# Overlapping the seams of a three-stage kernel: filter stage laid into the last spectrum pass, first parameter block laid into the last output pass

## The chip, the cores and the metric

One core of a Trainium2 chip runs the kernel. The metric is device microseconds of one execution. Engines are named as in the profile: PE is TensorE (PEld its weight loads), DVE VectorE, ACT ScalarE, POOL GpSimd, SP SyncE. A run counts as *slow* when it is over 1.5% above the fastest of the same kernel, else as *fast*.

## The reference, cut to what matters

The function mixes two branches of a sequence `x` of 2048 x 1024 by a gate and returns the output and all gradients.

```python
g = sigmoid((x * gate_w).sum(-1, keepdims=True))
a = irfft2(rfft2(x) * (w_r + 1j * w_i))                 # spectral branch
K = einsum("dn,dnl,dn->dl", C, exp(dt * A * l), dt * B).real
b = irfft(rfft(pad(x)) * rfft(pad(K)))[:L] + x * Dskip  # long convolution
out = g * a + (1 - g) * b
# returned: out and the gradients of x, w, A, B, C, log_dt, Dskip, gate_w for a given grad_out
```

The part of the kernel that the change touches has three stages. The *spectrum* of the convolution kernels is made in four passes, the last at about 875 to 905 us. The *filter* stage then runs over eight blocks of 128 channels: a second transform of the data, products with the spectrum, an inverse transform, one big transpose of the tile `Vt` into `Vr`, and an output pass. The *parameter* stage reduces the lag correlations that the filter stage left (`GKall`) to the gradients of A, B and C.

## The kernel before

The kernel is written with pools of buffers and a scheduler that orders each engine's instructions. Each engine is given its own list and waits on semaphores. The parts that matter, with cuts marked:

```python
# spectrum: all passes run with filler=None, the filter's pools open after the last one
if bi % 2 == 1:
    spectrum(bi // 2, Kc, K0, None)
...
for g0, g1 in ((0, 4), (4, 8), (8, 12), (12, 17)):       # 5.4 MB of tables, GpSimd's queue
    nc.gpsimd.dma_start(out=TKT[:, g0:g1]..., in_=tkt_scr[...])
...
def first(pr_, h, fp_, pool, tag, nb, eng):               # 24 of 64 are left for this stage
    if h % 2 == 0:
        xg = fp_.tile([P, 2, 2, 256], dt.bfloat16, name="xg", bufs=2)
        nc.sync.dma_start(out=xg[:, :, 0, :], in_=xv3[...])
        nc.sync.dma_start(out=xg[:, :, 1, :], in_=gbv[...])
    ...                                                   # 2 matmuls, one eviction to st, a store
...
sgs = {(0, g): load_s(0, g) for g in range(3)}
lts = {(0, hq): fetch(0, hq) for hq in range(4)}          # 12 output loads, 3.1 MB
for bi in range(DC):                                      # 8 filter blocks
    for g in range(NG):                                   # 5 groups
        nxt = second(...)                                 # group one ahead
        PY = products(g, *cur)
        firsts(1)
        lags(bi, *pend, pq)
        inverse(g, PY, Vt)
        firsts(1)
        last(bi - 1, Vr, g, ...)                          # outputs of the block before
    turn(Vr, Vt)                                          # the big transpose
for g in range(4):
    last(DC - 1, Vr, g, ...)
...                                                       # grad_s, pools closed, tail's pools opened
cur = blk_in(0)                                           # diagonal tile BD (4 copies on ACT)
for ch in range(4):
    blk_ch(0, ch, *cur)                                   # 16 matmuls, evictions to Tsb on ACT
load_par()                                                # four loads, the gate's row gwb last
for bi in range(DC):                                      # pd = Tsb * ORJ on DVE, pr = sums on PE
    ...
```

A *first* is the first transform of one slice of `x` and its gradient, two matmuls for a later block: Sync loads its input pair `xg`, its result is stored and read back as `Sg` by a *second*. `XG` is the output of a second, `PY` a product with the spectrum. `BD` is the diagonal tile made from one block of `GKall`; it is multiplied with four loaded chunks `A2t`, and an *eviction* copies each result out of TensorE's result memory (PSUM) to `Tsb`.

## Time and profile before

Median 1482.71 us of three runs (1478.46 to 1489.49); the span of the profiled execution, a further one, was 1489.8 (timed at 1491.57). I cut everything after the last small transpose of the lag rows (`KT<-Kq`) into four stretches, bounded by that transpose, the first and the last big transpose of the filter stage (`Vr<-Vt`), the first big product of the parameter stage (`pd`), and the end.

| stretch | us | what it holds |
|---|---|---|
| start of the program to the lag rows | 873.2 | not touched by the change |
| lag rows to first big transpose | 87.6 | first seam |
| first to last big transpose | 285.1 | seven filter blocks |
| last big transpose to first product | 59.5 | second seam |
| first product to end | 184.4 | the tail |

The same stretches in the busy times of the profile before (bounds, length, then busy time and instructions of PE, PEld, DVE, ACT, POOL; granted clock, DMA share, GB/s):

```profile
873.17:960.78 87.61, 61.75 (x422) 42.47 (x423) 36.22 (x82) 32.60 (x40) 15.84 (x17) 0.80 0.70 246
960.78:1245.87 285.09, 242.11 (x1726) 173.19 (x1725) 250.97 (x535) 162.70 (x270) 48.70 (x67) 0.92 0.74 144
1245.87:1305.40 59.53, 22.07 (x121) 12.58 (x119) 27.21 (x33) 31.16 (x60) 20.47 (x27) 0.65 0.88 254
1305.40:1489.80 184.40, 135.70 (x1200) 107.88 (x1199) 158.70 (x140) 114.65 (x153) 20.95 (x39) 0.90 0.53 177
```

Read DVE (third number) against the length: 36 of 88, 251 of 285, 27 of 60, 159 of 184. VectorE is nearly full in the second and fourth stretch, and the first and third, the seams, are mostly waiting. What a reordering can win lies mainly there.

### The profile page before, as it was taken

How to read it: one execution, taken by the hardware profiler on the slowest of the kernel's cores; microseconds unless marked ns; L12 is line 12 of the kernel's file. 1: busy time of each engine (PE TensorE's matmuls, PEld its weight loads, DVE VectorE, ACT ScalarE, POOL GpSimd, SP SyncE). 2: the span in 40 equal slices, each digit the busy share in tenths (PEclk: the TensorE clock that was granted, in tenths of full speed). 3: DMA queues.
4: the chain of work that ended last, by engine and by line, in shares of the span. 5: the costliest groups of instructions: out<-in, count | busy, mean ns of one | idle time of the engine just before them, and what ended most of it. 6: DMA issues, size and time to landing. Idle time of an engine off the chain costs nothing. (4 is left out here: it accounts for less than half of the span.)

```text
span 1489.8 us, 20203 instructions
## 1 busy us (share of the span) xinstructions
PE 1077.9 (72%) x7161; PEld 736.3 (49%) x7187; DVE 1133.5 (76%) x1883; ACT 857.4 (58%) x1321; POOL 237.8 (16%) x493
## 2 busy tenths in 40 slices
PE   3968887688790558757758773989888886387883
PEld 1434454344450445546546652656656654165672
DVE  5668998476628888687788853669989997378997
ACT  3553455433358785786784631757555554587860
POOL 4101100021243211010100104001212031321010
PEclk9979999899995557656858776989999998589996
DMA  4446574257535333344433538959986655877641
GB/s 148 152 139 157 154 233 151 100 118 117 83 129 224 117 132 133 116 157 168 154 124 120 184 106 310 268 128 171 190 143 161 84 187 76 316 248 258 205 148 29
DMA packets 153067, 236.06 MB, mean 158 GB/s; under 512 B 26371, under 2 KB 100739, under 8 KB 149766
## 3 DMA queue, kind: packets, MB, share of 16 engines
q1 hardware_dynamic: 133190, 179.37, 44.7%
q0 software_dynamic: 13536, 53.84, 10.4%
q10 hardware_dynamic: 6240, 1.57, 0.5%
q8 instruction: 56, 0.92, 0.3%
q14 instruction: 45, 0.37, 0.1%
HBM read 126.80 MB, written 107.66 MB: 157 GB/s over the span
## 5 line engine op out<-in xcount | busy, mean ns | idle before, releaser
L888 PE MATMUL pK<-wO,AN 128*128 128x84 bf16 x512 | 101.2, 344 | 24.3 <-DVE st L996 22.3
L1068 ACT ACTIVATE Vt<-f 128x1024 bf16<-128x1024 f32 (+1 forms) x72 | 64.4, 929 | 82.1 <-PE f L1157 44.9
L887 PE MATMUL trp<-ident,AN 128*128 128x128 bf16 x512 | 75.9, 275 | 47.8 <-DVE AN L817 41.5
L1309 ACT ACTIVATE Tsb<-pT 128x704 bf16<-128x704 f32 x128 | 88.0, 754 | 37.8 <-PE pT L1308 33.8
L1383 DVE TENSOR_TENSOR pd<-Tsb,ORJt 128x5376 bf16<-128x5376 bf16 x32 | 94.3, 2952 | 9.5 <-PE pr L1389 6.1
L923 PE MATMUL kx<-Kc,TK 128*128 128x256 bf16 x680 | 98.5, 291 | 0.7 <-DVE Kc L910 0.6
L888 PEld LDWEIGHTS <-AN 128*128 128x128 bf16 x512 | 75.6, 151 | 30.7 <-issue 25.3
L887 PEld LDWEIGHTS <-AN 128*128 128x128 bf16 x512 | 60.6, 158 | 55.5 <-DVE AN L817 42.9
L551 PE MATMUL p<-TD,UV 128*128 128x512 bf16 x240 | 66.9, 404 | 25.3 <-DVE Y L555 16.8
L1166 PE MATMUL pq<-TKT,PY 128*128 128x321 bf16 x544 | 83.7, 301 | 1.3 <-DVE PY L1136 1.0
L1308 PE MATMUL pT<-BD,A2t 128*128 128x176 bf16 x512 | 59.3, 251 | 31.3 <-ACT BD L1295 17.0
L1068 ACT ACTIVATE XG<-f 128x1024 bf16<-128x1024 f32 (+1 forms) x72 | 68.3, 984 | 19.7 <-PE f L1104 5.7
L1389 PE MATMUL pr<-pd,ident 128*128 128x256 bf16 x504 | 66.9, 281 | 16.9 <-DVE pd L1383 12.8
L923 PEld LDWEIGHTS <-TK 128*128 128x128 bf16 x680 | 64.1, 103 | 19.9 <-issue 2.6
L1123 DVE TENSOR_TENSOR m<-XG,kb 128x1024 bf16<-128x1024 bf16 (+1 forms) x80 | 47.0, 605 | 34.9 <-ACT XG L1068 21.0
L1193 PE MATMUL f<-Vr,S1i 128*128 128x256 bf16 x256 | 68.7, 391 | 4.2 <-DVE Vr L1074 4.2
L631 PE MATMUL p2i<-T,Z 128*128 128x512 bf16 x224 | 60.9, 394 | 12.8 <-DVE Z L598 5.9
L1308 PEld LDWEIGHTS <-A2t 128*128 128x128 bf16 x512 | 45.0, 102 | 49.1 <-issue 43.0
L1166 PEld LDWEIGHTS <-PY 128*128 128x128 bf16 x544 | 52.7, 98 | 25.2 <-DVE PY L1136 3.0
L996 DVE CAST st<-pK 128x1024 bf16<-128x1024 f32 x40 | 48.6, 1218 | 19.8 <-PE pK L991 19.7
L1389 PEld LDWEIGHTS <-ident 128*128 128x128 bf16 x504 | 49.3, 100 | 25.9 <-issue 11.6
L494 PE MATMUL p<-DP,UV 128*128 128x512 bf16 x250 | 61.1, 385 | 0.6 <-DVE UV L640 0.3
(829 smaller groups left out, 3160.7 us busy)
## 6 DMA issues: line engine op xcount, KB each, us to landing
at<-A SPq DMA_DIRECT2D x32, 512.0 KB
st<-st SPq DMA_DIRECT2D x64, 256.0 KB
A2t<-at SPq DMA_DIRECT2D x32, 512.0 KB
Sg<-st SPq DMA_DIRECT2D x24, 512.0 KB
on_scr<-OP SPq DMA_DIRECT2D x8, 1344.0 KB
ORJt<-on_scr POOLq DMA_DIRECT2D x8, 1344.0 KB, 8.9
spk<-spk SPq DMA_DIRECT2D x64, 128.0 KB
kb<-spk SPq DMA_DIRECT2D x32, 256.0 KB
```

Source lines behind the costliest of these rows:

```text
L494: nc.tensor.matmul(pd[:, eo, :], lhsT=V[:, eo * 2 + c_, b_, :, :].rearrange("p k n -> p (k n)")[:, h::H16], rhs=DP[:, eo * 2 + c_, b_, :], ...
L551: nc.tensor.matmul(ps[:, eo, :], lhsT=U[:, dc, (eo * K16 + k1r) * P:(eo * K16 + k1r + 1) * P], rhs=TD[:, dc, eo, :], start=(dc == 0), stop ...
L887: nc.tensor.transpose(trp[:, comp, cc, :], AN[:, comp, :, c], ident[:, :])
L888: nc.tensor.matmul(pK[:, c4, cc * 4 * NA:(cc + 1) * 4 * NA], lhsT=AN[:, comp, :, c], rhs=wO[:, comp, :, c::32].rearrange("p a q -> p q a") ...
L923: nc.tensor.matmul(px[:, comp, :], lhsT=TK[ci][:, k1, comp, :], rhs=Kc[:, ci, :], start=(ci == 0), stop=(ci == 4 and comp == 1))
L1068: nc.scalar.activation(out=out, in_=in_, func=ACT.Copy)
L1166: nc.tensor.matmul(pq[:, half, 0:NLG // 2], lhsT=PY[:, k_, comp, 256:384], rhs=TKT[:, p0 + k_, comp, half * (NLG // 2):(half + 1) * (NLG / ...
L1193: nc.tensor.matmul(py[:, hh, :, :], lhsT=S1i[:, f_, :], rhs=Vr[:, :, 2 * (hq * HQ + hh) + f_, :], start=False, stop=(f_ == 1), skip_group_ ...
L1308: nc.tensor.matmul(pT[:, cc, 0:4 * NX], lhsT=A2[:, comp, cl * N:(cl + 1) * N], rhs=BD[:, c0_ + cc, :, :].rearrange("p q x -> p (q x)"), st ...
L1309: nc.scalar.activation(out=Tsb[:, comp].rearrange("p x (q c) -> p x q c", q=4)[:, :, :, c0_:c0_ + 4], in_=pT[:, :, 0:4 * NX].rearrange("p ...
L1383: TT(out=pd[:], in0=Tsb[:, k_].rearrange("p (g a) d -> p g a d", g=2)[:, :, 0:NA, :], in1=O_.unsqueeze(1).to_broadcast([P, 2, NA, P]), op= ...
L1389: nc.tensor.matmul(pr[:], lhsT=idt[:], rhs=pd[:, :, a_, :], start=(k_ == 0 and a_ == 0), stop=(k_ == 1 and a_ == NA - 1))
```

## The change

The intent is to fill each seam with work of the next stage. Buffers of the filter stage go to the side of memory that is free earlier, so that block 0 can start between the matmuls of the last spectrum pass; the first parameter block goes between the last four output passes. The core of the diff:

```diff
-                if bi % 2 == 1:
+                if bi % 2 == 1 and more:
                     spectrum(bi // 2, Kc, K0, None)
...
-            fw = fctx.enter_context(tc.tile_pool(name="f_wk", bufs=2, reuse_waits="tile"))
+            fw = rctx.enter_context(tc.tile_pool(name="f_wk", bufs=2, side="right", reuse_waits="tile"))
...
+            def start_f():                                # called after each pair of spectrum rows
+                if n_ == 0:   second(0); load_s; load_t(0)
+                elif n_ == 2: second(1); products(0)
+                elif n_ == 5: load_s; load_t(1); second(2); products(1); inverse(0)
+                elif n_ == 7: load_s; load_t(2); load_t(3); second(3); products(2); inverse(1)
+            spectrum(NB2 - 1, Kc, K0, start_f)
...
-                    firsts(1)
+                    firsts(2 if i_ == 3 else 1)
...
-                    firsts(1)
...
+                    if bi == DC - 1:                      # was 16 accumulating copies on ACT
+                        nc.vector.tensor_reduce(out=ggall[:, pr_, hs], in_=gom[:], axis=AX.X, op=ALU.add)
...
+            cur = blk_in(0)
             for g in range(4):
                 last(DC - 1, Vr, g, lts[(NB2 - 1, g)])
+                blk_ch(0, g, *cur, psF, "f2", 3)
...
-            cur = blk_in(0)
-            for ch in range(4):
-                blk_ch(0, ch, *cur)
```

(`start_f` is shortened here.) Smaller parts: the tables are loaded by Sync in four pieces during the pass; one more `PY` buffer and one `Sg` buffer fewer; the twelve output loads are asked for after the pass; of the first parameter block, two of the four diagonal copies and half of the sixteen evictions are on VectorE instead of ScalarE.

## The prediction

> **What bounds the kernel now.** I read the page first (busy shares, the slices), then the busy times in chosen stretches, then the waits of two stretches, then single instructions in order of time. The page names no engine that is full:
>
> ```profile
> PE 1077.9 (72%) x7161; PEld 736.3 (49%) x7187; DVE 1133.5 (76%) x1883; ACT 857.4 (58%) x1321; POOL 237.8 (16%) x493
> DVE  5668998476628888687788853669989997378997
> ```
>
> The slices of VectorE are the message: 8 or 9 almost everywhere, and two dips, slices 24 and 25 (near 900 us) and 34 and 35 (near 1270 to 1300 us). These are the two seams that the change touches: last spectrum pass to filter stage, and last output pass to parameter stage. The stretches around them (columns: stretch, its length, busy time and instructions of TensorE, its weight loads, VectorE, ScalarE, GpSimd; then granted clock, DMA share, GB/s):
>
> ```profile
> 875.00:904.00 29.00, 26.58 (x188) 17.75 (x188) 6.28 (x11) 5.37 (x9) 2.10 (x1) 0.90 0.24 82
> 912.00:940.00 28.00, 9.04 (x52) 5.74 (x50) 12.92 (x28) 8.34 (x9) 5.96 (x8) 0.63 1.03 402
> 1010.00:1048.00 38.00, 34.80 (x257) 24.68 (x256) 35.56 (x76) 29.50 (x61) 6.70 (x10) 1.00 1.04 180
> 1209.00:1246.00 37.00, 31.33 (x227) 22.61 (x226) 34.37 (x75) 16.46 (x21) 6.51 (x9) 0.91 0.22 67
> 1265.00:1305.40 40.40, 13.71 (x72) 7.77 (x73) 15.06 (x15) 21.60 (x23) 14.65 (x19) 0.58 0.86 308
> 1350.00:1461.00 111.00, 90.02 (x820) 73.72 (x820) 106.08 (x87) 74.58 (x102) 9.71 (x18) 0.95 0.53 181
> ```
>
> The spectrum pass is TensorE alone (26.6 of 29 us) with VectorE idle; the 28 us after it have nobody busy and the DMA engines full; a steady filter block (1010 to 1048, 1209 to 1246) has VectorE at 93%; the 40 us before the parameter stage have nobody busy again; the body of that stage has VectorE at 96%. So outside the seams VectorE is the bound, at the seams waits are. What waits, first seam (904 to 962), then second (1240 to 1330):
>
> ```profile
> PE f L991 <- DMA xg<-gb_scr: 19.0, 2, 18.1
> DVE m L1123 <- ACT XG L1068: 18.0, 3, 14.5
> DVE m L1123 <- DMA Sg<-st: 9.8, 1, 9.8
> ```
>
> ```profile
> PE pT L1308 <- ACT BD L1295: 17.0, 1, 17.0
> PE pgg L1278 <- DMA xcf<-in_A_x_dram: 12.3, 5, 6.6
> DVE gxc L1275 <- DMA gxc<-gx_scr: 11.3, 4, 9.2
> ```
>
> Three single instructions bound the seams in time: the first transpose of a block, the last one, the first big product of the parameter stage.
>
> ```profile
> 960.78 4.50 DVE L1074 STREAM_TRANSPOSE Vr<-Vt 128x2048 f32<-128x2048 f32 x2
> 1245.87 4.50 DVE L1074 STREAM_TRANSPOSE Vr<-Vt 128x2048 f32<-128x2048 f32 x2 [0.34 <-ACT Vt L1068]
> 1305.40 2.96 DVE L1383 TENSOR_TENSOR pd<-Tsb,ORJt 128x5376 bf16<-128x5376 bf16 x1 [2.07 <-ACT Tsb L1309]
> ```
>
> From the last chunk (875) to the first transpose are 86 us; the eight transposes start at 960.8, 1010.2, 1048.0, 1088.8, 1128.7, 1167.9, 1208.6, 1245.9, so a block costs 39.3 us on average from the third on, and 49.4 the second; from the last transpose to the first product are 59.5 us; from there to the end of the span, 184.4.
>
> **What the Trainium skill says.** "TensorE: Matmul & The Clock Gate", Part 2, step by step: only weight loads are pulled ahead, matmuls stay in program order. The trace agrees: one matmul of the next filter input, placed at the head, waited 18.1 us for its load and everything behind it stood, VectorE 14.5 us of that. The same page, Part 1: after an idle window (about 3.4 us) the clock falls to half. It agrees: 0.50 granted from 920 to 930, where no matmul ran, 1.00 in busy blocks. "DMA: Bandwidth & Descriptors", issuing engines are not separate DMA queues: all issuers share the same 16 engines. It agrees: 402 GB/s at share 1.03 from 912 to 940, with GpSimd's table loads delaying loads issued by Sync. So moving the table loads to Sync's queue wins only by their new time, not by the queue. "VectorE: DVE Perf Modes", the perf-mode tier table: a reduction and fp32 from PSUM run at one element a cycle; here a 128x1024 cast from PSUM took 1.22 us and a 128x512 one 0.69.
>
> **The change part by part.** I compared the built orders of the two kernels: everything up to the last chunk is the same on every engine but for two loads on Sync's queue; the tile scheduler reorders only from 875 on.
>
> *Seam 1.* The filter stage's buffers now lie on the side that the earlier stage has freed, so the first four "second" groups, three product groups and two inverses of block 0 stand between the spectrum's matmuls. Nothing is removed: the work has to fit. TensorE until the first transpose: spectrum 26.6; five groups of 2 x 8 matmuls at 0.11 (start to start) 7; inverses 7.5; three of five lag groups at 2.2 (16 matmuls) 6.7; three "firsts" 1.3; sum 49, so 924 at the earliest, and with 4 to 5 us of waits (the cold first matmuls; two XG buffers that hold back the third group) about 929. VectorE until then: four product groups at 6.3 (911.3 to 917.6 in the trace), one small at 2.7, eight spectrum casts at 0.6, half a group of the next block 2.1: 35, from about 882.5 on: 918. So TensorE decides: **929 against 960.8, 32 us saved**. The 5.4 MB of tables are loaded during the pass, where the DMA share was 0.24, and the twelve gate and residual loads only after it, where before all met.
>
> *Blocks 1 to 7.* The two "firsts" of each group become one, so the 24 remaining spread to block 5 and not only to block 2. Block 1's extra 10 us before (7.5 of it ScalarE waiting for the store of such a tile) should mostly go. VectorE's work in a block is not changed: four groups 25.2, small 2.7, transpose 4.4, outputs 5.2 = 37.5. Seven blocks at 39.6, plus 2 for what stays of the stall: 279 against 285.1, **6 saved**: last transpose at 1208.
>
> *Seam 2.* The first parameter block's chunks go between the four last outputs, and the gate's matmuls and loads no longer stand in front of them. Before, the block's diagonal tile began only after grad_s: zeroing at 1265.0, matmuls at 1275.4, then stalls on the x loads. Now it begins when the transpose ends. VectorE's work from there to the first product, in its new order: zeroing 2.4; four transposes 3.9; three multiplies 2.6; four outputs (0.69 + 0.42 + 0.69) 7.2; four reductions of 1024, estimated at 1.2 from the cast of 1024, 4.8; two diagonal copies, estimated at 0.6 each; eight PSUM copies of 704, 0.88 between the two casts above, 7.0; scalars 0.3: sum 29.4, less about 2.5 since neighbours overlap by 0.07. With 3 to 4 us of waits and the transpose itself, 4.5, the first product is 35 us after the last transpose: **24.5 saved**. ScalarE has half of this to do (16 accumulating activations, 9.4 us with their reads, are gone; 2 of 4 diagonal copies of 1.37 and 8 of 16 evictions of 0.75 too), so it runs ahead into block 1.
>
> *The rest.* VectorE has 158.7 us of work after the first product, and the change pushes into it four gate updates (5.1), a multiply (0.9) and one more (0.7): 6.7. Against it, 6 to 8 us of the 11 that VectorE idled before 1350, where ScalarE was the bound (39.7 of 44.6) or the gate loads were late, should go, ScalarE being ahead by three diagonal copies and about six evictions (8.6). Net zero: 184, which I shade to 183.
>
> Sum in the profile's time: 1208 + 35 + 183 = 1426, against 1489.8: 64 less, 4.3%. The timed median is 1482.7, the profiled execution was a long one, so **1420 us**.
>
> **The rivals.**
> 1. *TensorE's order becomes the trap.* Inverses stand in front of spectrum matmuls and wait for products; ScalarE's third XG eviction waits for a buffer, and the spectrum's evictions stand behind it. For it: this very form cost 18.1 us before. Against it: the products are 11 us ahead of TensorE in my count. If half the gain of the seam goes: 1436.
> 2. *The load is only moved.* The table, output and xg loads still collide, now at 905 to 925. For it: 5.4 MB plus 3.1 MB need over 20 us at 402 GB/s whoever issues them; the output loads wait for the pass to end. Against it: 30 us of a nearly idle DMA lie in front. It would give back 5 to 10 us: 1425 to 1430.
> 3. *VectorE gives the tail back.* It takes copies from ScalarE while it is the bound. The 13 us of copies and reductions are in my sum; if its waits add up (three PSUM buffers shared by outputs and chunks, gate loads late for the moved updates), the first product is at +45 and the rest 192: 1445.
> 4. *Better still.* The seam closes to VectorE's 918 and no stalls stay: 1405.
>
> **Range and chances.** Rivals 1 to 3 seldom all come; their sum would be near 1465. Range 1400 to 1446. The line for "faster" by over 2% is 1453: chance 0.94; within 2% 0.05; slower 0.01, since nothing but about 15 us of VectorE work is added and it lies in stretches idle by 60%.
>
> **What would show it.** The first transpose near 929 (later than 945: seam 1 failed; look for TensorE waiting for PY or xg there). Blocks of 39 to 40 us; over 42 means that spread "firsts" cost. The first big product 35 us after the last transpose; the wait of pT for BD gone from 17 us to a few. GB/s over 150 in the spectrum pass. Last, 180 to 188 us from the first product to the end. The prediction is wrong if VectorE's busy share does not rise from 76% to about 79 or 80%.

## The result, and the profile after

The changed kernel took 1440.98 us (median of 4 runs, 1435.44 to 1445.4) against 1483.95 (4 runs, 1478.46 to 1489.49) of the kernel before on the same chip. A ratio is the mean time of one kernel's fast runs over that of the other's of the same rounds, so not quite the ratio of these medians: 0.9708, with a 95% interval of 0.9657 to 0.976. Run again on another chip the same kernel gave 0.9758 (0.9677 to 0.984). So 2.4 to 2.9% faster; the first interval lies wholly below 0.98, the second reaches past it, so that run alone does not settle a gain of over 2%. The direction is as predicted, the time 21 us longer than predicted, inside the range.

The page of the profile after, VectorE's share and its slices:

```profile
PE 1070.7 (74%) x7161; PEld 736.9 (51%) x7187; DVE 1143.5 (80%) x1897; ACT 841.8 (59%) x1279; POOL 239.2 (17%) x489
DVE  5668999667726979788878887388999999789997
```

The share rose from 76 to 80%, and the dip of the second seam is gone from the row. Of the first a narrower one is left (the 7 3 near the 26th slice). The four stretches, cut at the same instructions:

```profile
864.44:935.38 70.94, 58.26 (x410) 40.77 (x411) 35.57 (x82) 26.73 (x34) 13.67 (x13) 0.87 0.81 267
935.38:1209.57 274.19, 241.46 (x1737) 172.63 (x1736) 251.02 (x534) 167.71 (x276) 48.84 (x67) 0.95 0.76 160
1209.57:1246.17 36.60, 18.73 (x122) 13.84 (x120) 31.17 (x37) 19.54 (x21) 13.56 (x14) 0.66 0.90 192
1246.17:1437.50 191.33, 142.01 (x1201) 110.86 (x1199) 164.98 (x151) 111.45 (x151) 28.16 (x53) 0.88 0.62 212
```

Look first at the bounds: the lag rows come at 864.4 here and came at 873.2 before. The instructions up to there are the same in both kernels, so 8.7 of the 52.3 us between the two profiled spans are not the change. Two repeats, one of each kernel, show how large such differences are:

| stretch, us | before | before, repeat | after | after, repeat | predicted |
|---|---|---|---|---|---|
| start to the lag rows | 873.2 | 869.3 | 864.4 | 880.0 | as before |
| first seam | 87.6 | 88.2 | 70.9 | 69.5 | 55.8 |
| seven blocks | 285.1 | 278.4 | 274.2 | 286.4 | 279 |
| second seam | 59.5 | 62.9 | 36.6 | 38.6 | 35 |
| tail | 184.4 | 184.3 | 191.3 | 190.1 | 183 |

(The predicted first seam is the predicted 929 less the 873.2 of the profile before. The repeat of the kernel before was a single run, so its state is unknown; its clock, 0.826, and time are those of the fast runs beside it.) The unchanged first part and the seven blocks vary by 10 us and more between executions of one kernel. The seams and the tail agree within 3.4 us between the two profiles of a kernel. On the means: the first seam won 17.7 us, the second 23.6, the tail gave back 6.4, and the blocks moved by 1.5, which is nothing against their spread. Together 36 us, 2.4% of some 1485, in accord with the timed ratios.

The first seam is where most of the prediction went missing. TensorE in the changed kernel, single instructions (start, duration, instruction, in brackets the idle time before it and what ended it), and under it the issues of the loads it stood for:

```profile
920.79 1.89 PE L992 MATMUL f<-xg,S1f 128*128 128x512 bf16 x4 [5.45 <-DMA xg<-gb_scr]
...
930.78 0.84 PE L992 MATMUL f<-xg,S1f 128*128 128x512 bf16 x2 [4.12 <-DMA xg<-gb_scr]
```

```profile
912.74 0.46 SPq L987 DMA_DIRECT2D xg<-gb_scr  x1
...
916.48 1.10 SPq L987 DMA_DIRECT2D xg<-gb_scr  x1
```

Both waits stand in front of inverse transforms that the big transpose needs. The loads were issued 8 and 14 us before the matmuls began, while in the quiet part of the program the median from issue to landing of these loads is 2.3 us.

### The profile page after: what moved, and what is told of

It reads as the page before. It is cut to its first block, busy times and chain, and to the rows that moved or that the text cites. A ratio compares the mean times of both kernels' runs of the same rounds, so it can differ in the third digit from the quotient of the medians.

```text
span 1437.5 us, 20147 instructions
## 1 busy us (share of the span) xinstructions
PE 1070.7 (74%) x7161; PEld 736.9 (51%) x7187; DVE 1143.5 (80%) x1897; ACT 841.8 (59%) x1279; POOL 239.2 (17%) x489
## 3 DMA queue, kind: packets, MB, share of 16 engines
q0 software_dynamic: 12960, 48.25, 10.9%
## 5 line engine op out<-in xcount | busy, mean ns | idle before, releaser
L1434 DVE TENSOR_TENSOR pd<-Tsb,ORJ 128x5376 bf16<-128x5376 bf16 x32 | 94.0, 2949 | 8.2 <-PE pr L1440 7.0
L1321 ACT ACTIVATE Tsb<-pT 128x704 bf16<-128x704 f32 x112 | 76.7, 754 | 26.2 <-PE pT L1315 26.0
L1440 PE MATMUL pr<-pd,ident 128*128 128x256 bf16 x504 | 70.6, 292 | 16.4 <-DVE pd L1434 16.3
L629 PE MATMUL p2i<-T,Z 128*128 128x512 bf16 x224 | 60.4, 390 | 9.8 <-DVE Z L596 4.4
L1315 PEld LDWEIGHTS <-A2t 128*128 128x128 bf16 x512 | 47.3, 105 | 38.3 <-issue 25.7
L997 DVE CAST st<-pK 128x1024 bf16<-128x1024 f32 x40 | 48.6, 1218 | 19.7 <-PE pK L992 19.5
L1315 PE MATMUL pT<-BD,A2t 128*128 128x176 bf16 x448 | 52.0, 251 | 12.8 <-ACT Tsb L1321 7.5
```

Source lines behind the costliest of these rows:

```text
L1315: nc.tensor.matmul(pT[:, cc, 0:4 * NX], lhsT=A2[:, comp, cl * N:(cl + 1) * N], rhs=BD[:, c0_ + cc, :, :].rearrange("p q x -> p (q x)"), st ...
L1321: nc.scalar.activation(out=to_, in_=ti_, func=ACT.Copy)
L1434: TT(out=pd[:], in0=Tsb[:, k_].rearrange("p (g a) d -> p g a d", g=2)[:, :, 0:NA, :], in1=O_.unsqueeze(1).to_broadcast([P, 2, NA, P]), op= ...
L1440: nc.tensor.matmul(pr[:], lhsT=idt[:], rhs=pd[:, :, a_, :], start=(k_ == 0 and a_ == 0), stop=(k_ == 1 and a_ == NA - 1))
```

## The experiments

**1. Each half alone.** `head_only` takes the changed first seam and the tail of the kernel before:

```diff
-            rctx.close()
-            te = ...                       # early pool, blk_in(0), blk_ch between the outputs
+            for g in range(4):
+                last(DC - 1, Vr, g, lts[(NB2 - 1, g)])
+            ...                            # the tail of the kernel before, sums on ACT
```

> The changed first seam (filter stage interleaved with the spectrum pass, firsts spread) with the tail of the kernel before. If the two seams add up independently: first transpose at 935 as in the changed kernel, last transpose at 1209 to 1211, from there 59.5 to the first big product and 184.4 to the end as in the kernel before, so a span near 1454, 36 us (2.4%) below the kernel before. If the seams interact (the tail's ScalarE sums or the gate's loads reach back into the filter stage): the last transpose later than 1213, or the tail not 244 us long but 3 us or more off.

`tail_only` is the kernel before with the changed tail; `f_last` holds what the last outputs need, so that the rest can be freed for the early pool:

```diff
+            fl = fctx.enter_context(tc.tile_pool(name="f_last", bufs=2, reuse_waits="tile"))
-            for g in range(4):
-                last(DC - 1, Vr, g, ...)
-            ...
+            te = ...                       # early pool, blk_in(0), blk_ch between the outputs
```

> The first seam of the kernel before with the changed tail. If additive: first transpose near 961, last near 1246, first big product 36 to 37 us later, end 191 us after that: span near 1474, 16 us (1.1%) below the kernel before. If the 7 us that the changed kernel gave back after the first big product came from something that the first seam left behind, the last part is 184 to 186 and the span near 1467.

`head_only` took 1464.11 us, ratio 0.9917 (0.9875 to 0.9959), a gain of 0.8% where 2.4% was expected (the expectation had counted as gain the 8.7 us before the lag rows and the 10.9 us of the blocks, which the repeats show to be within the spread); `tail_only` 1466.31 (one of its four runs slow and left out of the ratio), ratio 0.9901 (0.9852 to 0.995). The stretches of `head_only`: 70.7, 274.8, 65.6, 180.2, span 1459.0, 5 us above the additive sum: 3.3 of it came before the lag rows, the second seam was longer than in either profile before, the tail 4 us shorter. The profiled execution of `tail_only` was slow and its stretches are not used. The two gains, 0.8 and 1.0%, add to 1.8%; the change gave 2.4 to 2.9% with intervals of about half a per cent each. The halves fall short of the whole by 0.6 to 1.1%, about what the intervals allow, so these runs neither show nor exclude that the seams help each other.

**2. Without the firsts in block 0.** `firsts_late`:

```diff
-                    firsts(2 if i_ == 3 else 1)
+                    firsts(0 if i_ < 5 else (2 if i_ in (5, 6, 7) else 1))
```

> The changed kernel without the three or four firsts in the first filter block (their count is made up in the second, two per group). If the 6 us that the first seam lacked against the prediction (first transpose 935.4, predicted 929) are TensorE standing for the xg loads (5.5 and 4.1 us, in front of inverses): first transpose at 926 to 930, the second block 1 to 3 us longer for its added firsts, last transpose near 1204, span 4 to 7 us below the changed kernel. Rival, that the block is held by the PY and spk buffers or by VectorE: first transpose at 933 or later and no gain.

The first seam fell to 58.6 us (first transpose at 925.2, expected at 926 to 930), and the kernel was slower all the same: 1448.4 us, ratio 0.9807 (0.9756 to 0.9858), against 1436.33 for `fetch_late` below, which behaves as the changed kernel and ran on the same chip. The first seam of this run, and the largest PE wait of the block behind it:

```profile
866.63:925.22 58.59, 54.92 (x408) 40.02 (x409) 35.85 (x82) 24.16 (x31) 13.68 (x13) 0.90 0.82 271
```

```profile
PE f L992 <- DMA xg<-gb_scr: 18.5, 1, 18.5
```

The wait moved into the second block and grew: that block took 57.4 us where the changed kernel took 40.3, and the load landed 23.8 us after its issue. The expectation of 1 to 3 us for the second block was wrong. What follows: the firsts, with the wait for their loads, cost the seam about 12 us, and moving them is no cure. (The profile has one more loss, a wait of VectorE of 6.2 us in the last block put down to "remote". Waits of that name, 2.6 to 5.0 us each, also stand in the blocks of `before_again`, `after_again`, `xg_ahead` and `sums_act`, and none in the three profiles of the changed filter stage whose blocks took 274 to 275 us. What they are is not known.)

**3. The output loads, first try and second.** Is the xg load late because it is issued late, or because 3.1 MB of output loads are in flight? `fetch_late` moved these loads behind the first big transpose in the program:

```diff
-                    for hq in range(4):
-                        lts[(0, hq)] = fetch(0, hq)
...
                 turn(Vr, Vt)
+                if bi == 0:
+                    for hq in range(4):
+                        lts[(0, hq)] = fetch(0, hq)
```

> The changed kernel with the twelve loads of the output stage (3.1 MB) issued after the first transpose, all else the same. If the xg loads are late because they share the DMA engines with these: TensorE's wait for xg falls from 9.6 us to under 4, the first transpose comes at 929 to 931, but the first outputs may wait up to 5 us for their loads, so the span is between 5 us less and equal. If xg is late because its load is issued late (912 to 917, behind other work on Sync's queue) the wait stays over 7 us and the first transpose stays at 934 to 936.

The run answers nothing (the wait for xg stayed at 9.9 us): GpSimd had no reason to wait and issued the loads at 922 to 933 us, before the transpose at 946.0, as the changed kernel does. The place in the program is not an order in time. Since the filter stage is then that of the changed kernel, it serves as a third look at it: 71.0, 274.3, 33.9, 189.5 us, and 1436.33 us, ratio 0.9726 (0.9678 to 0.9774).

`fetch_hold` gives the loads a reason to wait, a copy from the transposed tile into each buffer:

```diff
+                    if pr_ == 0:
+                        nc.gpsimd.tensor_copy(out=t_[:, 0, 0:2], in_=held[0][:, 0, 0, :])   # held[0] is Vr
                     nc.gpsimd.dma_start(out=t_[:], in_=src[:, hs, csl])
```

> The changed kernel with the twelve output loads (3.1 MB) really held back: GpSimd first copies two columns of the turned tile into each buffer, so that they start only after the first big transpose (in the run before this was tried by place in the program alone, and the loads stayed where they were). If xg lands late because these loads share the DMA engines: its two waits fall from 9.6 us to under 5 and the first seam takes 62 to 66 in place of 70.9; the second block then waits 8 to 14 us for the held loads, so the span is no better. If only the late issue on Sync's queue matters: the first seam stays at 69 to 72.

The first seam and the wait for xg in it:

```profile
866.60:926.30 59.70, 55.45 (x416) 39.99 (x417) 35.53 (x81) 26.75 (x34) 4.79 (x1) 0.93 0.80 265
```

```profile
PE f L992 <- DMA xg<-gb_scr: 0.9, 1, 0.9
```

The wait went from 9.6 us to 0.9 and the seam to 59.7, with the firsts in their places and xg issued as late as in the changed kernel (914.7, 48 us after the lag rows in both). So the output loads in flight were what made xg late, not its own late issue. The price came as expected in kind and larger in size: the first outputs waited 20.3 us, the second block took 59.0 us, and the kernel 1457.63 (0.9828, 0.9768 to 0.9889).

**4. xg loaded two pairs ahead.** `xg_ahead` keeps everything in place and issues the loads of the firsts earlier, the first two pairs before the spectrum pass, in the same two buffers:

```diff
+            for n_ in (0, 2):                         # before the last spectrum pass
+                xpre[fq[n_]] = load_x(*fq[n_], fw)
...
-                    xg = fp_.tile(...); nc.sync.dma_start(...); nc.sync.dma_start(...)
+                    xg = xpre.pop((pr_, h), None) or load_x(pr_, h, fp_)
...
+                    if done[1] % 2 == 1 and len(fq) > 2:   # a pair is used up: load the one after next
+                        xpre[fq[2]] = load_x(*fq[2], fw)
```

> The changed kernel with the loads of the firsts' inputs (xg) issued two pairs ahead, the first two before the spectrum pass, in the same two buffers. Firsts and their places are kept. If the first seam lacks its gain because TensorE stands in order for xg: from the last transpose of the lag rows to the first big transpose 58 to 61 us in place of 70.9 (it was 58.6 without firsts in the first block), blocks 1 to 7 unchanged at 273 to 276, so 10 to 13 us (0.7 to 0.9%) off the changed kernel. If the DMA engines' load is the cause and any load issued then comes late: another load (Sg, kb or the tables) takes the wait over, and that stretch stays above 66.

1447.58 us, ratio 0.9656 (0.9578 to 0.9733). Beside it on the same chip ran the changed kernel:

> The changed kernel unchanged, on this chip, beside the others. If the stretches from the last lag rows on are steady and only the unchanged first part of the program varies: 70 to 72, 273 to 275, 35 to 38 and 189 to 193 us for the four stretches (to the first big transpose, to the last, to the first big product, to the end), whatever the span; the start of the first stretch anywhere from 864 to 875.

1461.17 us, ratio 0.9758, with the stretches of the table above: first seam, second seam and tail came within 0.6 us of what was expected, the start (880.0) and the seven blocks (286.4) did not. The chip's runs were longer altogether (1495.65 for the kernel before). The first seam of `xg_ahead` took 60.4 us against 69.5, and no wait for xg is left in it:

```profile
868.52:928.95 60.43, 55.28 (x416) 40.26 (x417) 36.56 (x83) 27.01 (x34) 13.67 (x13) 0.93 0.82 271
```

TensorE is busy 55.3 of 60.4 us: the seam is now mostly TensorE's own work. The waits for xg had cost more than their length: in the profile after, TensorE was busy 58.3 us for fewer matmuls (410 against 416), at a granted clock of 0.87 in place of 0.93, and the six matmuls behind the two waits took a median of 0.63 us where the kernel's median for that form is 0.38. The seven blocks took 288.8 us, beside 286.4 for the changed kernel on this chip, and the tail 195.0. The medians differ by 0.9%, as expected from the seam, though the two intervals overlap.

**5. ScalarE or VectorE in the second seam.** `copies_act` gives the ten copies that went to VectorE back to ScalarE:

```diff
-                    if bi == 0 and q % 2 == 0:
+                    if False:
...
-                        if bi == 0 and comp == 1:
+                        if False:
```

> The changed kernel with the ten copies of the first parameter block that it gave to VectorE (two of the diagonal tile, eight evictions of Tsb) back on ScalarE. If VectorE bounds the stretch from the last big transpose to the first big product (31.4 us busy of 36.6): that stretch shortens by 4 to 8 us and the rest stays at 191, a net gain of 3 to 8. If ScalarE's chain (diagonal, evictions) sets it: ScalarE has 8.7 us more to do, the stretch is 36 to 42 us, and the rest 191 to 196 because ScalarE is no longer ahead.

`sums_act` gives the four reductions back as sixteen accumulating copies:

```diff
-                    if bi == DC - 1:
-                        nc.vector.tensor_reduce(out=ggall[:, pr_, hs], in_=gom[:], axis=AX.X, op=ALU.add)
-                    for hh in range(HQ if bi < DC - 1 else 0):
+                    for hh in range(HQ):
```

> The changed kernel with the four reductions of the last outputs (4.8 us of VectorE) back as sixteen accumulating copies on ScalarE (9 to 10 us). If VectorE bounds the stretch to the first big product: 2 to 5 us shorter there. If the two engines are near balance: within 2 us of the changed kernel; and if ScalarE sets the tail's start, 3 to 6 us longer.

In `copies_act` VectorE had 25.6 us of work in the second seam in place of 31.2, and the seam took 36.5: no gain at all. In `sums_act` it took 36.8. So VectorE's sum is not the only thing that sets this seam. In `copies_act` VectorE waited for the diagonal's chain instead (diagonal, matmuls, evictions; TensorE stood 8.7 us for the diagonal, 5.9 in the changed kernel): work taken off VectorE lengthened a chain through ScalarE that is about as long. Neither run takes work off VectorE without giving it to ScalarE, so VectorE is not ruled out as a bound.

The other profiles with the changed tail say more. The same code took 34.0 us in `fetch_late`, `fetch_hold` and `firsts_two` (and in `best`, with one later load moved), 34.8 in `xg_ahead`, 36.0 in `firsts_late`, 36.6 and 38.6 in the two profiles of the changed kernel. Below, the second seam of `copies_act` and of `fetch_late`, and one instruction of TensorE in the changed kernel and in `fetch_late`:

```profile
1216.85:1253.32 36.47, 17.51 (x114) 12.36 (x111) 25.64 (x31) 23.92 (x29) 12.91 (x13) 0.69 0.89 175
1220.36:1254.35 33.99, 17.04 (x114) 12.26 (x111) 31.00 (x38) 20.04 (x22) 13.10 (x13) 0.67 0.88 199
```

```profile
1240.67 0.78 PE L1315 MATMUL f<-BD,A2t 128*128 128x176 bf16 x8 [3.42 <-DMA A2t<-at]
1248.62 0.78 PE L1316 MATMUL f<-BD,A2t 128*128 128x176 bf16 x8 [0.57 <-DMA A2t<-at]
```

TensorE waits for the chunk `A2t` 3.4 us in the changed kernel, 5.1 in its repeat, 0.6 in `fetch_late`, and VectorE's wait for TensorE's chunks goes with it: 3.4, 5.3, 0.9. With that wait short, VectorE is busy 31.0 of 34.0 us. It is the pattern of the first seam again, a load in front of TensorE, though no run here was made to remove it.

The tail took 203.6 and 201.6 us, more than any theory had given it. In `copies_act` most of it is one wait of VectorE, 1.9 us in the changed kernel (waited for, sum, times, longest), and the queue of SyncE shows where it comes from:

```profile
DVE gxc L1367 <- DMA gwb<-in_gate_w_dram: 10.3, 1, 10.3
```

```profile
1235.16 18.14 SPq L1308 DMA_DIRECT2D A2t<-at  x4
...
1262.99 0.83 SPq L1353 DMA_DIRECT2D gwb<-in_gate_w_dram  x1
```

The gate's row is issued behind loads of `A2t` that wait for one of three buffers; with the evictions late, these came free late, the row was issued at 1263.0 and landed 14.9 us later, and the gate update that needs it stood in VectorE's order ahead of the next products. In the changed kernel it is issued 7.5 us after the first product, here 9.7 after it, and lands in 10.9 us there; so 2 us of the delay are the late issue and 4 a slower landing. In `sums_act` no single wait explains it; the waits for pr, gxc, Tsb and gwb in its tail sum to 23.5 us, in the changed kernel's to 14.8. Timed, `copies_act` is no different from the changed kernel on that chip (1461.77, 0.9762 with 0.9695 to 0.9828): its blocks were 6 us shorter in the profile. `sums_act` is 12 us slower (1473.16, 0.9835 with 0.9775 to 0.9895).

**6. The kernel before again, and two firsts per group.**

> The kernel before, unchanged, on another chip, for its stretches from the last transpose of the lag rows on. If the stretches of the first profile are typical: 87.6, 285.1, 59.5 and 184.4 us, each within 2. If its second block (49.4) or the waits of its first seam were partly a matter of that one execution, as the smaller gain in the timed runs suggests: the sum from the lag rows on is 606 to 612 in place of 616.6.

The repeat (1484.92 us) is in the table: the first seam and the tail repeat, the second seam is 3.4 us longer, so the sum from the lag rows on, 613.8, meets neither theory. The second block took 41.8 us where the first profile had 49.4: the stall on which the prediction built a saving is not there in the second execution.

`firsts_two` undoes the spreading of the firsts:

```diff
-                    firsts(2 if i_ == 3 else 1)
+                    firsts(2)
```

> The changed kernel with two firsts per group as in the kernel before, instead of one. If the spread firsts are what took the extra 10 us out of the second block: the first seam at 71 to 76, blocks 1 to 7 at 280 to 287 in place of 274 (the second block 46 to 52), span 6 to 14 us above the changed kernel. If the second block was slow before only because the first seam was in disorder there: 273 to 277 as in the changed kernel and no loss.

1445.71 us, ratio 0.9755 (0.97 to 0.9809); first seam 71.3, seven blocks 283.8. This lies between the 274 and 286 of the changed kernel's own profiles, so neither theory is shown: if the spreading is worth anything, it is less than the blocks vary by.

**7. A version from what was learnt.** `best` is `xg_ahead` with the gate's row as the first of the four parameter loads:

```diff
             def load_par():
+                nc.sync.dma_start(out=gwb2[:], in_=gate_w.partition_broadcast(P))
                 nc.sync.dma_start(out=parT_[:], in_=nlb_scr[:].rearrange("r p d -> p r d"))
...
-                nc.sync.dma_start(out=gwb2[:], in_=gate_w.partition_broadcast(P))
```

> The changed kernel with xg loaded two pairs ahead, and the gate's weight row as the first of the four parameter loads in place of the last. First seam 59 to 62, blocks 273 to 283 by the chip, second seam 35 to 37, and the rest 188 to 193: 1.9 us of waiting for the gate row gone if the two gate updates there do not then wait for another load. 10 to 13 us below the changed kernel, ratio to the kernel before 0.960 to 0.968. Rival: the gate row only takes the place of the parameter loads behind it, and the rest stays at 191 to 195; the gain is then the first seam's alone.

1436.04 us (6 runs), ratio 0.9688 (0.9643 to 0.9734): below the kernel before; beside the changed kernel's 0.9708 and 0.9758 on other chips the difference is not resolved by the timing. Its stretches:

```profile
876.06:935.96 59.90, 54.88 (x416) 40.05 (x417) 36.55 (x83) 27.00 (x34) 13.67 (x13) 0.94 0.84 273
935.96:1214.54 278.58, 241.78 (x1731) 171.97 (x1730) 250.22 (x534) 167.07 (x275) 48.75 (x67) 0.95 0.80 167
1214.54:1248.50 33.96, 17.23 (x118) 12.40 (x116) 30.97 (x37) 20.02 (x22) 13.07 (x13) 0.70 0.88 198
1248.50:1440.10 191.60, 142.83 (x1206) 111.22 (x1204) 165.14 (x151) 110.89 (x150) 28.59 (x53) 0.88 0.62 214
```

The first seam repeats at 59.9; the ratio is just outside the expected 0.960 to 0.968. The tail did not move: the 1.9 us of waiting for the gate's row went, and 2.0 us for `dt_b`, now the last of the four loads, came. That was the rival named for this run.

## Why the prediction was right or wrong

*That the waits at the seams, not an engine, are what the change takes away*: right for the first seam, which shrank with nearly the same work in it (VectorE 36.2 and 35.6 us). In the second it is only part: ScalarE's work there fell from 31.2 to 19.5 us, and the gate's updates went to the tail, so the net gain of seam and tail together is 17.2 us. Moving copies or sums back to ScalarE left the seam as it was, so the gain is not owed to that exchange; how much of it comes from the earlier start of the diagonal tile and how much from the gate's work having left was not tested.

*First seam, 32 us saved*: wrong, 17.7 on the means. The first transpose at 935.4 looks like a miss of 6 us only because the unchanged part ended 8.7 us earlier in that execution; counted from the lag rows the miss is 15.1. The step that failed is the allowance of "4 to 5 us of waits" on top of TensorE's sum: it held no wait for xg. About 11 us of the miss are the xg loads, shown three ways: without the firsts 58.6, with the output loads held back 59.7, with xg loaded ahead 60.4 and 59.9. It is what the prediction had as its second rival, "the load is only moved", at 5 to 10 us, and had set aside because 30 us of idle DMA lie in front; but the output loads cannot use those, since they are issued after the pass. The prediction leaned on the Trainium skill, "DMA: Bandwidth & Descriptors", § Issuing engines are not separate DMA queues, for the tables alone. `fetch_hold` agrees with it for the output loads too: with GpSimd's transfers held back, TensorE's wait for Sync's loads fell from 9.6 us to 0.9. The remaining 4 us are TensorE's sum: it counted three of five lag groups in this stretch, 48 matmuls; 68 run in it, and 20 more at 0.15 us (2.4 us for 16 in the trace) are an estimated 3 us. (A slip in the same sum: five groups of 16 matmuls at 0.11 would be 8.8 us and not 7; with the fifth group a quarter of the size, as `GRP` has it, they are 7.5. And "1.00 in busy blocks" holds for one of the two blocks that it shows; the other has 0.91.)

*Blocks 1 to 7, 6 us saved by spreading the firsts*: not shown. The sum of 279 lies between the two profiles after, but the stall it rested on was gone in the repeat of the kernel before, and undoing the spreading changed nothing outside the spread.

*Second seam, 24.5 us saved*: right in size, 23.6. The sum of VectorE's work was right too, 31.2 us measured where 29.4 less 2.5 plus 4.5 makes 31.4. What the reasoning lacked is a second chain of about the same length, the diagonal's through ScalarE and TensorE (with 5.5 us moved there from VectorE the seam was just as long), and the wait for `A2t`: the seam lay between 34.0 and 38.6 us in step with it.

*The tail, net zero*: wrong, 6.4 us longer. The term of added work was right: VectorE is busy 164.98 us there in place of 158.70, 6.3 more where 6.7 was written. The term that failed is the 6 to 8 us of idle time that should have gone against it: VectorE idled 25.7 us before and 26.4 after. In the first 44.6 us after the first product, where the prediction had found its 11 us, it idled 11.1 before and 10.4 after. That stretch and VectorE's waits in it, in the kernel before and then in the changed one:

```profile
1305.40:1350.00 44.60, 38.09 (x332) 29.55 (x332) 33.55 (x18) 39.69 (x51) 10.70 (x20) 0.94 0.77 256
1246.17:1290.77 44.60, 37.56 (x311) 29.96 (x310) 34.20 (x25) 33.55 (x46) 8.14 (x16) 0.86 0.89 323
```

```profile
DVE gxc L1275 <- DMA gxc<-gx_scr: 4.1, 2, 2.9
DVE pd L1383 <- ACT Tsb L1309: 3.0, 3, 2.1
DVE pd L1383 <- PE pr L1389: 2.9, 1, 2.9
```

```profile
DVE pd L1434 <- PE pr L1440: 3.9, 1, 3.9
DVE gxc L1367 <- DMA gxc<-gx_scr: 3.4, 1, 3.4
DVE gxc L1367 <- DMA gwb<-in_gate_w_dram: 1.9, 1, 1.9
DVE pd L1434 <- ACT Tsb L1321: 1.1, 1, 1.1
```

ScalarE did get ahead, with 33.6 us of work there in place of 39.7. The wait for ScalarE did shrink, from 3.0 to 1.1. It had never been more than 3; the rest was TensorE's sums and the gate's loads, and ScalarE being ahead does nothing for those. The third rival had the tail at 192, which is what came. Of its reasons, gate loads late for the moved updates are seen (the 3.4 and 1.9 us above); that the copies taken from ScalarE cost it is not, since giving them back did not shorten the tail. Why TensorE's sums are waited for longer in single pieces (3.9 us; the granted clock was 0.66 in the stretch before) was not tested.

*The time*: 1420 predicted, 1441 measured. In the terms of the table the misses on the means are 14.4 and 2.6 us at the seams, 7.7 in the tail and 1.3 in the blocks, 26 together. All four go one way, so that the time stays inside the range, by 5 us, is owed to the range's width and not to terms that cancel. Of the signs that the prediction named, VectorE's share (80%), the wait for BD (17.0 us to 5.9) and the traffic in the spectrum pass (251 GB/s in its 29 us) came; the tail of 180 to 188 did not.

## What to carry to other kernels

Before filling an idle stretch with the next stage, list every load that the moved work needs and every load issued in that stretch, because a small load in front of an in-order TensorE costs its landing time under that burst and not its quiet one; the cure is to issue it earlier in a spare buffer, not to move its consumer. Compare stretches bounded by the same instructions instead of absolute times, and profile the kernel before twice before building a saving on one stall in it. A dependency, not the place in the program, decides when a load is issued, and one load that waits for a buffer holds up everything behind it in that queue.

## What the Trainium skill lacked or had wrong

- "DMA: Bandwidth & Descriptors", § Anatomy of one DMA — SWDGE (gpsimd) path: its fit, 2.0 us and the bytes at 436 GB/s, gives an estimated 2.3 us for one 128 KB xg load; it is stated for GpSimd's path, and Sync's loads of that size landed in a median of 2.3 us in the quiet part. It has no term for other transfers in flight: the same load took up to 23.8 us with the output loads around it.
- No page that I read gives the spread between executions of one kernel: the same instructions took 864.4 to 880.0 us up to the lag rows in fast runs, and seven equal filter blocks 274.2 to 286.4, while both seams and the tail repeated within 3.4 us (the second seam within 4.6 over all profiles with the changed tail).
- "TensorE: Matmul & The Clock Gate", Part 2, step by step, has that matmuls keep program order, and no size for what a wait at their head costs. Here two groups of matmuls, 2.7 us together, stood 9.6 us for loads, and the seam was 9 to 12 us shorter without that.
